# Weights loaded later, rows interleaved and heads finished one by one in a decode attention kernel

## The chip, the core and the metric

The kernel runs on one core of one Trainium2 chip. The metric is the device time of one execution in microseconds (us); the profile calls the stretch from the first to the last instruction the span. A median is taken over repeated runs, and a change counts as faster or slower when it moves the time by over 2%. In the profile PE is the matmul engine (PEld its weight loads), DVE the vector engine, ACT the scalar engine, SP the engine that issues most of the transfers, and a trailing q (DVEq, SPq) an engine's sequencer. L266 is line 266 of the kernel that is profiled, so the same operation has another line number in each variant.

## The reference

For each of two rows the output is the input, plus attention of one query token over a cache of 8192 keys in 32 heads of width 128, plus a gated MLP (gMLP). Inputs and outputs are bf16.

```python
# x (2,1,512); k_cache, v_cache (2,32,8192,128); wq (512,4096); wo (4096,512)
# w_in (512,1792); w_out (896,512)
xn = _layernorm(x)
q = heads(xn @ wq)
p = _softmax(einsum('bhqd,bhkd->bhqk', q, k_cache) * 128 ** -0.5)
attn = merge(einsum('bhqk,bhkd->bhqd', p, v_cache)) @ wo
z = _gelu(xn @ w_in);  z1, z2 = z[..., :896], _layernorm(z[..., 896:])
mlp = (z1 * (w_sp * z2 + b_sp)) @ w_out
out = x + attn + mlp
```

## The kernel before

Each head reads a K tile and a V tile of 2.10 MB each. DVE multiplies the whole K tile by the query, which stands broadcast in all partitions (`qbc`), and adds halves of the head dimension together, six times on the tile and once more into `s_t`. ACT takes the exponential, and PE multiplies by V in 64 small matmuls. The row is the outer loop, and the output projection waits for the end of each row. Below, heads are counted from 0 to 63 in the order in which they are worked on; `h` is the head index within a row.

```python
kpool = ctx.enter_context(tc.tile_pool(name="kpool", bufs=3))
vpool = ctx.enter_context(tc.tile_pool(name="vpool", bufs=2))
spool = ctx.enter_context(tc.tile_pool(name="spool", bufs=3))
# ... cut: wq chunks and the K/V pairs of heads 0 and 1 on the SyncE queue ...
nc.gpsimd.dma_start(w_in_sb[:], ...)      # 1.8 MB
nc.gpsimd.dma_start(w_out_sb[:], ...)     # 0.9 MB
nc.gpsimd.dma_start(wo_sb[:], ...)        # 4.2 MB, all heads
# ... cut: layer norm of x, helpers make_q and make_gmlp ...
make_q(0)
for b in range(B):
    o_ps = psum_ob.tile([P, H], F32, name="o_ps")
    for h in range(H):
        # ... cut: kt, vt = issue_kv(b, h), or the pair loaded ahead ...
        nc.vector.tensor_tensor(out=kt[:], in0=kt[:], in1=q_bcast, op=ALU.mult)
        w = Dh
        while w > 2:                      # six halving adds
            hw = w // 2
            nc.vector.tensor_tensor(out=kt[:, :, 0:hw], in0=kt[:, :, 0:hw],
                                    in1=kt[:, :, hw:w], op=ALU.add)
            w = hw
        s_t = spool.tile([P, J], F32, name="s_t")
        nc.vector.tensor_tensor(out=s_t[:].unsqueeze(2), in0=kt[:, :, 0:1],
                                in1=kt[:, :, 1:2], op=ALU.add)   # "the small add"
        e_t = spool.tile([P, J], BF16, name="e_t")
        nc.scalar.activation(out=e_t[:], in_=s_t[:], func=ACT.Exp, scale=SCALE,
                             accum_out=l_all[:, gh:gh + 1])
        for j in range(J):                # 64 value matmuls
            nc.tensor.matmul(o_ps[:, h:h + 1], lhsT=vt[:, j, :], rhs=e_t[:, j:j + 1], ...)
        if not prologue_done and (h >= 3 or h == H - 1):
            # ... cut: make_q of the other row, make_gmlp() ...
    # one block per row: sum over partitions, reciprocal, scaling,
    nc.tensor.matmul(l_ps[:], lhsT=ones_f[:], rhs=l_all[:, b * H:(b + 1) * H], ...)
    nc.vector.reciprocal(out=lr[:], in_=l_ps[:])
    nc.vector.tensor_tensor(out=o_sb[:, b, :], in0=o_ps[:], in1=lr[:], op=ALU.mult)
    # 7 matmuls with w_out, 32 with wo, the residual and the store
    # ... cut ...
```

The softmax here doesn't subtract the row's maximum and nothing guards it: scores larger than these inputs give would overflow.

## Time and profile before

| | kernel before |
|---|---|
| time, median (lowest to highest) of 6 runs | 727.93 us (724.26 to 729.3) |
| span of the profiled run (its time was 724.26) | 722.5 us |
| DVE busy | 641.7 us, 89% |
| multiply of one head, 128x8192 | 4.42 us |
| head to head, early / late | 10.15 / 10.21 us |

The prediction below shows the busy shares, the costliest groups, the timeline of DVE and the stretches. One further view helps. It is from the page: it divides the span into 40 equal slices, and gives DVE's busy share of each in tenths and the rate of the transfers.

```profile
DVE  2248899999999999999989899999999999999991
...
GB/s 304 356 390 283 424 429 429 426 427 427 415 403 411 422 421 385 423 423 402 403 409 208 432 424 433 424 430 422 399 408 412 414 414 409 405 424 401 418 228 0
```

DVE is idle for much of the first three slices (54 us) and in the last one.

### The profile page before, as it was taken

How to read it: one execution, taken by the hardware profiler on the slowest of the kernel's cores; microseconds unless marked ns; L12 is line 12 of the kernel's file. 1: busy time of each engine (PE TensorE's matmuls, PEld its weight loads, DVE VectorE, ACT ScalarE, POOL GpSimd, SP SyncE). 2: the span in 40 equal slices, each digit the busy share in tenths (PEclk: the TensorE clock that was granted, in tenths of full speed). 3: DMA queues.
4: the chain of work that ended last, by engine and by line, in shares of the span. 5: the costliest groups of instructions: out<-in, count | busy, mean ns of one | idle time of the engine just before them, and what ended most of it. 6: DMA issues, size and time to landing. Idle time of an engine off the chain costs nothing.

```text
span 722.5 us, 9759 instructions
## 1 busy us (share of the span) xinstructions
PE 163.1 (23%) x4303; PEld 133.2 (18%) x4304; DVE 641.7 (89%) x558; ACT 37.5 (5%) x151; POOL 5.4 (1%) x13
## 2 busy tenths in 40 slices
PE   0228412221222112211235221222112211222126
PEld 0004212221112112211222221221111111111012
DVE  2248899999999999999989899999999999999991
ACT  0004100000000000000000000000000000000000
POOL 2000000000000000000000000000000000000000
PEclk9999555555555555555557555555555555555557
DMA  7997999999999999999995999999999999999950
GB/s 304 356 390 283 424 429 429 426 427 427 415 403 411 422 421 385 423 423 402 403 409 208 432 424 433 424 430 422 399 408 412 414 414 409 405 424 401 418 228 0
DMA packets 24326, 280.21 MB, mean 388 GB/s; under 512 B 2294, under 2 KB 6396, under 8 KB 7900
## 3 DMA queue, kind: packets, MB, share of 16 engines
q1 hardware_dynamic: 22668, 272.64, 91.2%
q0 software_dynamic: 1616, 6.95, 2.7%
q8 instruction: 33, 0.54, 0.3%
q14 instruction: 9, 0.07, 0.0%
HBM read 279.58 MB, written 0.00 MB: 387 GB/s over the span
## 4 chain that ended last, share of the span: by engine, by line
DVE 80%; DMA 8%; PE 5%; SPq 4%; issue 2%; ACT 0%; DVEq 0%; ACTq 0%
DVE kt L270 43%; DVE kt L266 35%; DMA kt<-in_A_k_cache_dram 4%; DMA wq_sb<-in_A_wq_dram 4%; PE out_ps L311 2%; DVE s_t L275 2%; SPq L72 2%; PE q_ps L173 2%; SPq L81 1%; PE o_ps L284 1%; SPq L83 0%; DVE res L317 0%; ACT L279 0%; DVEq L275 0%; PE l_ps L295 0%
## 5 line engine op out<-in xcount | busy, mean ns | idle before, releaser
L270 DVE TENSOR_TENSOR kt<-kt 128x4096 bf16<-128x4096 bf16 (+5 forms) x384 | 335.6, 877 | 12.3
L266 DVE TENSOR_TENSOR kt<-kt,qbc 128x8192 bf16<-128x8192 bf16 x64 | 282.8, 4418 | 34.0 <-DMA kt<-in_A_k_cache_dram 22.1
L284 PE MATMUL o_ps<-e_t,vt 128*128 128x1 bf16 x4096 | 117.8, 165 | 509.0 <-ACT e_t L279 509.0
L284 PEld LDWEIGHTS <-vt 128*128 128x128 bf16 x4096 | 116.2, 104 | 512.4 <-issue 471.3
L279 ACT ACTIVATE e_t<-s_t 128x64 bf16<-128x64 f32 x64 | 16.4, 256 | 600.1 <-DVE s_t L275 600.1
L173 PE MATMUL q_ps<-wq_sb,xn_rep 128*128 128x512 bf16 x63 | 19.7, 470 | 22.5 <-DMA wq_sb<-in_A_wq_dram 22.4
L275 DVE TENSOR_TENSOR s_t<-kt 128x64 f32<-128x64 bf16 x64 | 19.1, 299 | 6.0
L311 PE MATMUL out_ps<-wo_sb,o_sb 128*1 128x512 bf16 x64 | 17.6, 443 | 1.4 <-DVE o_sb L299 1.4
L173 PEld LDWEIGHTS <-xn_rep 128*128 128x128 bf16 x64 | 6.6, 111 | 34.0 <-DMA wq_sb<-in_A_wq_dram 20.9
L279 ACT ACTIVATION_READ_ACCUMULATOR e_t<-s_t 128x1 f32 x64 | 11.9, 186 | 0.0
L177 ACT CAST qbc<-q_ps 128x512 bf16<-128x512 f32 x16 | 9.4, 585 | 46.5 <-PE q_ps L173 46.5
L317 DVE TENSOR_TENSOR res<-out_ps,x_b 1x512 bf16<-1x512 f32 x2 | 1.4, 678 | 9.8 <-PE out_ps L311 9.8
L311 PEld LDWEIGHTS <-o_sb 128*1 128x1 bf16 x64 | 5.9, 94 | 12.3 <-issue 5.1
L298 DVE RECIPROCAL lr<-l_ps 128x32 f32<-128x32 f32 x2 | 0.7, 358 | 5.7 <-PE l_ps L295 5.7
L305 PE MATMUL out_ps<-w_out_sb,hT 128*1 128x512 bf16 x14 | 4.8, 501 | 1.7 <-DVE hT L249 0.9
L184 PE MATMUL zst_ps<-xnT,w_in_sb 128*128 128x2 bf16 x56 | 1.9, 165 | 10.3 <-DMA w_in_sb<-in_B_w_in_dram 10.3
L184 PEld LDWEIGHTS <-w_in_sb 128*128 128x128 bf16 x56 | 1.8, 100 | 11.1 <-DMA w_in_sb<-in_B_w_in_dram 10.4
L279 ACT ACT_TABLE_LOAD x2 | 2.6, 1283 | 13.6 <-DVE s_t L275 13.6
L157 PE MATMUL zst_ps<-ident,xn_rows 2*128 2x2 f32 x4 | 0.6, 238 | 11.5 <-DVE xn_rows L147 11.5
L157 PEld LDWEIGHTS zst_ps<-ident,xn_rows 2*128 2x128 f32 x4 | 0.5, 208 | 11.5 <-issue 11.5
L233 DVE CAST wsp_f<-wsp_sb 128x1 f32<-128x1 bf16 x1 | 0.2, 154 | 2.5 <-DMA wsp_sb<-in_B_w_sp_dram 2.5
L124 DVE CAST x_f<-x_rows 2x512 f32<-2x512 bf16 x1 | 0.4, 415 | 2.1 <-DMA x_rows<-in_A_x_dram 2.1
(54 smaller groups left out, 21.9 us busy)
## 6 DMA issues: line engine op xcount, KB each, us to landing
kt<-in_A_k_cache_dram SPq DMA_DIRECT2D x64, 2048.0 KB, 14.7
vt<-in_A_v_cache_dram SPq DMA_DIRECT2D x64, 2048.0 KB, 9.5
wq_sb<-in_A_wq_dram SPq DMA_DIRECT2D x8, 512.0 KB, 22.4
wo_sb<-in_A_wo_dram POOLq DMA_DIRECT2D x1, 4096.0 KB, 36.4
w_in_sb<-in_B_w_in_dram POOLq DMA_DIRECT2D x1, 1792.0 KB, 19.8
w_out_sb<-in_B_w_out_dram POOLq DMA_DIRECT2D x1, 896.0 KB, 22.4
x_b<-in_A_x_dram SPq DMA_DIRECT2D x2, 1.0 KB
out_dram<-res SPq DMA_DIRECT2D x2, 1.0 KB
```

The costliest lines, as they stand in the source:

```text
L72: nc.sync.dma_start(wq_sb[:, :, c * NQ:(c + 1) * NQ], A_wq[:, c * NQ:(c + 1) * NQ].rearrange("(k p) n -> p k n", p=P),)
L81: nc.sync.dma_start(kt[:], A_k_cache[b, h].rearrange("(p j) d -> p j d", p=P))
L173: nc.tensor.matmul(q_ps[:], lhsT=xn_rep[:, b, k, :], rhs=wq_sb[:, k, c * NQ:(c + 1) * NQ], start=(k == 0), stop=(k == KD - 1),)
L177: nc.scalar.copy(out=qbc[b][:, c * NQ:(c + 1) * NQ], in_=q_ps[:])
L184: nc.tensor.matmul(z_ps[:, c, :], lhsT=w_in_sb[:, k, c * P:(c + 1) * P], rhs=xnT[:, k, :], start=(k == 0), stop=(k == KD - 1),)
L266: nc.vector.tensor_tensor(out=kt[:], in0=kt[:], in1=q_bcast, op=ALU.mult)
L270: nc.vector.tensor_tensor(out=kt[:, :, 0:hw], in0=kt[:, :, 0:hw], in1=kt[:, :, hw:w], op=ALU.add)
L275: nc.vector.tensor_tensor(out=s_t[:].unsqueeze(2), in0=kt[:, :, 0:1], in1=kt[:, :, 1:2], op=ALU.add)
L279: nc.scalar.activation(out=e_t[:], in_=s_t[:], func=ACT.Exp, scale=SCALE, accum_out=l_all[:, gh:gh + 1],)
L284: nc.tensor.matmul(o_ps[:, h:h + 1], lhsT=vt[:, j, :], rhs=e_t[:, j:j + 1], start=(j == 0), stop=(j == J - 1),)
L305: nc.tensor.matmul(out_ps[:], lhsT=hT[:, c, b:b + 1], rhs=w_out_sb[:, c, :], start=(idx == 0), stop=(idx == n_mm - 1),)
L311: nc.tensor.matmul(out_ps[:], lhsT=o_sb[:, b, h:h + 1], rhs=wo_sb[:, h, :], start=(idx == 0), stop=(idx == n_mm - 1),)
```

## The change

The intent is to take from the start what it doesn't need, and to spread the work of the tail over the heads:

1. `w_in` and `w_out` are no longer loaded at the start but at heads 4 and 8 of the loop, and `wo` comes as one tile of 131 KB per head index, all on the SyncE queue.
2. The head is the outer loop and the row the inner one; a query chunk is made for both rows at once.
3. K has four buffers instead of three, V three instead of two.
4. Each head is finished by itself under the multiply of the next: one matmul for the sum, a reciprocal of 128x1 on DVE, a scaling on ACT, one output matmul. Only seven `w_out` matmuls per row are left for the end.
5. DVE runs in program order (`manual_schedule`), where before the scheduler chose. The gMLP stands ahead of the two heads of h = 8.

```diff
-    kpool = ctx.enter_context(tc.tile_pool(name="kpool", bufs=3))
-    vpool = ctx.enter_context(tc.tile_pool(name="vpool", bufs=2))
+    kpool = ctx.enter_context(tc.tile_pool(name="kpool", bufs=4))
+    vpool = ctx.enter_context(tc.tile_pool(name="vpool", bufs=3))
+    wpool = ctx.enter_context(tc.tile_pool(name="wpool", bufs=3))
 ... cut ...
+    def issue_wo(h):
+        wt = wpool.tile([P, N_OUT], BF16, name="wot")
+        nc.sync.dma_start(wt[:], A_wo[h * Dh:(h + 1) * Dh, :])
+        return wt
 ... cut: order of the first loads ...
-    nc.gpsimd.dma_start(w_in_sb[:], B_w_in.rearrange("(k p) f -> p k f", p=P))
-    nc.gpsimd.dma_start(w_out_sb[:], B_w_out.rearrange("(c p) n -> p c n", p=P))
-    wo_sb = const.tile([P, H, N_OUT], BF16, name="wo_sb")
-    nc.gpsimd.dma_start(wo_sb[:], A_wo.rearrange("(h p) n -> p h n", p=P))
+    def issue_w_in_dma():
+        nc.sync.dma_start(w_in_sb[:], B_w_in.rearrange("(k p) f -> p k f", p=P))
+    def issue_w_out_dma():
+        nc.sync.dma_start(w_out_sb[:], B_w_out.rearrange("(c p) n -> p c n", p=P))
 ... cut ...
+    def finish_head(st, last):
+        b_, h_, gh_, hps_, wo_t_, out_ps_, first_ = st
+        rl = work.tile([P, 1], F32, name="rl")
+        nc.vector.reciprocal(out=rl[:], in_=hps_[:, 1:2])
+        nc.scalar.activation(out=o_sb[:, gh_:gh_ + 1], in_=hps_[:, 0:1], func=ACT.Copy,
+                             scale=rl[:, 0:1])
+        nc.tensor.matmul(
+            out_ps_[:], lhsT=o_sb[:, gh_:gh_ + 1], rhs=wo_t_[:],
+            start=first_, stop=False,
+        )
 ... cut: finish_row, the 7 w_out matmuls, residual and store ...
+    with tc.manual_schedule(engines={mybir.EngineType.DVE}):
         for h in range(H):
+            for b in range(B):
 ... cut ...
+                if b == 0 and h == 8:
+                    issue_w_out_dma()
+                if b == 0 and h == 4:
+                    issue_w_in_dma()
+                if b == 0 and h == 8:
+                    make_gmlp()
+                    prox.close()
+                nc.vector.tensor_tensor(out=kt[:], in0=kt[:], in1=q_bcast, op=ALU.mult)
+                if prev is not None:
+                    finish_head(prev, False)
 ... cut: the six adds, the small add, exp and value matmuls as before ...
+                nc.tensor.matmul(hps[:, 1:2], lhsT=ones_f[:], rhs=l_all[:, gh:gh + 1],
+                                 start=True, stop=True)
+        finish_head(prev, True)
+        finish_row(1, out_pss[1])
```

## The prediction

> **What bounds the kernel now.** I read the page's busy shares first, then the groups of instructions, then VectorE (DVE) in order of time, and last the DMA rate of single stretches.
>
> ```profile
> PE 163.1 (23%) x4303; PEld 133.2 (18%) x4304; DVE 641.7 (89%) x558; ACT 37.5 (5%) x151; POOL 5.4 (1%) x13
> ...
> L270 DVE TENSOR_TENSOR kt<-kt 128x4096 bf16<-128x4096 bf16 (+5 forms) x384 | 335.6, 877 | 12.3
> L266 DVE TENSOR_TENSOR kt<-kt,qbc 128x8192 bf16<-128x8192 bf16 x64 | 282.8, 4418 | 34.0 <-DMA kt<-in_A_k_cache_dram 22.1
> ```
>
> DVE works 641.7 of 722.5 us, nearly all of it on 64 equal heads (one multiply of 4.42 us, six halving adds, one last small add). The change leaves this work alone, so the 81 us in which DVE idles are the most that it could win. The timeline of DVE shows where the large idle pieces lie:
>
> ```profile
> 12.30 1.17 DVE L163 COPY xn_rep<-xnT 128x128 bf16<-128x128 bf16 x8
> 25.39 4.42 DVE L266 TENSOR_TENSOR kt<-kt,qbc 128x8192 bf16<-128x8192 bf16 x1 [11.92 <-ACT qbc L177]
> 46.34 4.42 DVE L266 TENSOR_TENSOR kt<-kt,qbc 128x8192 bf16<-128x8192 bf16 x1 [16.52 <-DMA kt<-in_A_k_cache_dram]
> 50.68 9.58 DVE L270 TENSOR_TENSOR kt<-kt 128x4096 bf16<-128x4096 bf16 x12
> 60.17 0.51 DVE L275 TENSOR_TENSOR s_t<-kt 128x64 f32<-128x64 bf16 x2
> 63.18 4.43 DVE L266 TENSOR_TENSOR kt<-kt,qbc 128x8192 bf16<-128x8192 bf16 x1 [2.50 <-DMA kt<-in_A_k_cache_dram]
> ...
> 706.53 0.30 DVE L275 TENSOR_TENSOR s_t<-kt 128x64 f32<-128x64 bf16 x1
> 709.68 0.36 DVE L298 RECIPROCAL lr<-l_ps 128x32 f32<-128x32 f32 x1 [2.85 <-PE l_ps L295]
> 710.07 0.19 DVE L299 TENSOR_TENSOR o_sb<-o_ps,lr 128x32 bf16<-128x32 f32 x1
> 719.57 0.68 DVE L317 TENSOR_TENSOR res<-out_ps,x_b 1x512 bf16<-1x512 f32 x1 [9.31 <-PE out_ps L311]
> ```
>
> Three pieces are to be seen. The start: the scheduler interleaved heads 0 and 1, head 0's adds stand behind head 1's multiply, that one waits for its K tile until 46.34, and the third multiply starts only at 63.18. The end: 15.7 us lie between the last add (706.83) and the end of the span, 9.2 of them 32 output matmuls in a row. In between all is steady: multiplies start 10.15 us apart (98.45 to 108.60) and later 10.21 (686.33 to 696.54). From 63.18 to 706.83 are 643.7 us; 62 heads at 10.21 are 633, so only 11 us are lost in the long middle: the gMLP, the change of row at 374 (about 4) and three short waits for K.
>
> The stretches (PE, PEld, DVE, ACT, POOL busy, then clock, DMA share, GB/s) show how close DMA is:
>
> ```profile
> 98.45:190.34 91.89, 16.60 (x576) 16.59 (x576) 89.25 (x74) 4.42 (x19) 0.00 (x0) 0.50 1.01 428
> 200.55:363.91 163.36, 29.53 (x1024) 29.02 (x1024) 158.42 (x129) 5.59 (x32) 0.00 (x0) 0.50 1.00 410
> 20.00:40.00 20.00, 6.09 (x29) 1.87 (x29) 4.42 (x1) 1.75 (x3) 0.00 (x0) 1.00 1.04 351
> 48.00:56.00 8.00, 3.21 (x9) 1.21 (x10) 8.00 (x4) 0.58 (x1) 0.00 (x0) 1.00 1.05 365
> ```
>
> While DMA catches up it moves 428 GB/s; once DVE sets the pace it moves what is asked for, 4.19 MB in 10.21 us, 410. Where wq and wo are loaded (rows of 1 KB) it falls to about 350. DVE is the bound, DMA a close second.
>
> **The Trainium skill.** *HBM Reference*, Specifications, puts a core streaming alone at about 425 GB/s; the trace agrees (428). *DMA: Bandwidth & Descriptors*, Specifications, gives 512 B as the smallest transfer for line rate; this trace does not bear that out for the 1 KB rows, 351 and 365 GB/s. *Perfetto Trace Analysis*, Optimization Strategy, says that consistent bubbles can mean too few buffers. The trace has none: the multiply waited for K four times in 64. So deeper pools alone should earn little. *VectorE: DVE Perf Modes*, The perf-mode tier table, has bf16 tensor_tensor capped at two elements per cycle; 8192 in 4.42 us agree with that at the 0.96 GHz of its Specifications, so the heads' time stays.
>
> **The change part by part.**
>
> *Start.* DVE now follows program order, so head 0 is not held by head 1. The queries come chunk by chunk for both rows, and w_in, w_out and wo leave the start for later. What then counts is the third K tile, behind two K/V pairs, all of wq (4.19 MB) and one wo tile: five 2.10 MB tiles at 428 GB/s, 24.5 us, and 4.3 MB of 1 KB rows. For the latter I take 315 GB/s: in the packet records a 1 KB packet takes about 52 ns, times 16 engines. That is 13.7 us. Data flow from about 5.3 us (1.18 MB had moved by 8.0), so the tile is there near 44. The same sum for the second K tile of the kernel before gives 46, and it came at 46.34. Heads 0 and 1 fit in ahead (start near 12, then K at 23.5, done by 34), and DVE waits some 10 us. Third multiply at 44 instead of 63.2: 19 us won.
>
> *A head in the middle.* Added per head: one reciprocal of 128x1, which by the rows of 128x2 (166 ns) takes about 0.16 us, 64 of them 10 us of busy time. It stands between the multiply and the first add. In the kernel before a copy of 0.18 us stood in the same place once (z_sb, 67.52) and the first add began 4.46 us after the multiply's start, exactly as without it. So I count zero, at most 0.06 for its second wait. The matmuls of the previous head must be through: exp, one matmul for the sum and 1.85 us of value matmuls end about 3 us into the head, the reciprocal asks at 4.4. ACT and PE have room. Taken: 10.18 us a head, 62 heads, 631 us.
>
> *gMLP.* It now stands on DVE as one block of 22 small operations ahead of head 16. The kernel before took 4.2 us from zsig to hT; with the five ahead of them, the exp round trip and two casts I take 6 us.
>
> *DMA in the middle.* Two heads need four tiles and one 131 KB wo tile: 19.6 + 0.4 us, 10.0 a head against 10.18. At head 2 DMA has no lead, by head 9 1.3 us, then w_in costs 4.4: DVE waits 3 us. The gMLP gives 6 back before w_out asks for 3. K now goes out three heads ahead, so no further wait.
>
> *Change of row.* Gone, 4 us; it is in the 11 us that I replace.
>
> *Tail.* Of 39 output matmuls, 8 stay behind the last head: 0.5 (exp) + 0.5 (sum) + 1.85 + 0.2 (reciprocal) + 0.4 (ACT) + 8 x 0.43 + 0.7 (residual) + 2.3 (store) = 10, instead of 15.7.
>
> Sum: 44 + 631 + 3 + 6 + 10 = 694 us of span. The median of the runs lay 5.4 us above the profiled span (727.93 against 722.5); I add 6: 700 us.
>
> **The rivals.** First: DMA becomes the bound. At 410 GB/s instead of 428 a head takes 10.4 us of DMA; then 61 heads from 44, w_in, w_out, one head on DVE and the tail give 44 + 636 + 7 + 10 + 10 = 707 of span, 712 in time. Against it: whenever DMA had a backlog it held 427 to 428 over some 100 us, twice. Second: the reciprocal makes DVE wait for PE and ACT in each head, say 0.3 us, 19 us in all: 718, a gain within 2%. The margin of 1.4 us at a granted clock of 0.50 speaks against it. Third: the early part is slower, because PE does all query chunks before head 1's value matmuls, so that the reciprocal in head 2 asks at 48.8 what PE gives near 47; a slip of a few us at most. Fourth: the 1 KB rows move at 365, and the third K tile comes at 42: 698.
>
> **Range and chances.** The start and the tail are arithmetic on measured rates and hold to 3 or 4 us each; the middle can only grow, by 0.1 us a head for every 1% of DMA. So 690 to 711. Faster by over 2% means below 713.4: 0.93; within 2% 0.06; slower 0.01.
>
> **What would show it.** Right: third multiply at 42 to 47, released by DMA; multiplies 10.15 to 10.25 apart; idle ahead of the reciprocals near zero; one DVE wait of some us near head 9; 10 us from last add to end. Wrong: DMA waits ahead of multiplies all through, then DMA is the bound; PE or ACT as releaser of the reciprocals, then the second rival; a third multiply after 50.

## The result and the profile after

| | before | after |
|---|---|---|
| time, median (lowest to highest) | 728.32 us (724.26 to 729.97), 16 runs | 694.07 us (693.59 to 694.26), 8 runs |
| profiled span | 722.5 us | 692.2 us |
| third multiply starts | 63.18 us | 44.27 us |
| third multiply to end of last small add | 643.65 us | 638.07 us |
| end of last small add to end of span | 15.7 us | 9.86 us |

The changed kernel takes 0.9535 of the time, with a 95% interval of 0.9517 to 0.9552. Such a ratio is the mean time of one kernel's fast runs over that of the other's in the same rounds, so it is not quite the ratio of the medians quoted.

The last three rows of the table divide the 30.3 us by which the span shrank: 18.9 at the start, 5.6 in the middle and 5.8 in the tail. (The medians differ by 34.3 us, because the profiled run of the kernel before was its fastest.)

The page of the kernel after gives these shares and DVE groups. A group's line gives busy time, the mean ns of one, and after the second bar the idle time ahead of it with what ended most of it.

```profile
PE 213.4 (31%) x4427; PEld 157.6 (23%) x4428; DVE 645.4 (93%) x618; ACT 54.3 (8%) x215; POOL 2.5 (0%) x11
...
L320 DVE TENSOR_TENSOR kt<-kt 128x4096 bf16<-128x4096 bf16 (+5 forms) x384 | 336.9, 877 | 11.0
L313 DVE TENSOR_TENSOR kt<-kt,qbc 128x8192 bf16<-128x8192 bf16 x64 | 282.8, 4418 | 18.3 <-DMA kt<-in_A_k_cache_dram 15.0
...
L274 DVE RECIPROCAL rl<-hps 128x1 f32<-128x1 f32 x64 | 10.2, 160 | 2.3 <-PE hps L339 2.3
```

Each multiply and add lasts what it lasted before. The idle time ahead of the multiplies fell from 34.0 to 18.3 us. The new reciprocals add 10.2 us of busy time, yet DVE is busy only 3.7 us longer, as records that overlap are counted once. The timeline of DVE, with start, duration and, in brackets, the wait before it, shows the start, the wait at head 9, two heads of the steady part and the tail:

```profile
23.61 4.42 DVE L313 TENSOR_TENSOR kt<-kt,qbc 128x8192 bf16<-128x8192 bf16 x1 [1.05 <-DMA kt<-in_A_k_cache_dram]
...
44.27 4.43 DVE L313 TENSOR_TENSOR kt<-kt,qbc 128x8192 bf16<-128x8192 bf16 x1 [10.42 <-DMA kt<-in_A_k_cache_dram]
48.61 0.16 DVE L274 RECIPROCAL rl<-hps 128x1 f32<-128x1 f32 x1
...
118.84 4.42 DVE L313 TENSOR_TENSOR kt<-kt,qbc 128x8192 bf16<-128x8192 bf16 x1 [3.50 <-DMA kt<-in_A_k_cache_dram]
...
226.06 4.42 DVE L313 TENSOR_TENSOR kt<-kt,qbc 128x8192 bf16<-128x8192 bf16 x1
...
236.20 4.42 DVE L313 TENSOR_TENSOR kt<-kt,qbc 128x8192 bf16<-128x8192 bf16 x1
240.53 0.16 DVE L274 RECIPROCAL rl<-hps 128x1 f32<-128x1 f32 x1
240.65 5.43 DVE L320 TENSOR_TENSOR kt<-kt 128x4096 bf16<-128x4096 bf16 x6
...
682.04 0.30 DVE L325 TENSOR_TENSOR s_t<-kt 128x64 f32<-128x64 bf16 x1
...
685.24 0.17 DVE L274 RECIPROCAL rl<-hps 128x1 f32<-128x1 f32 x1 [2.31 <-PE hps L339]
689.36 0.68 DVE L289 TENSOR_TENSOR res<-out_ps,x_b 1x512 bf16<-1x512 f32 x1 [3.96 <-PE out_ps L284]
```

The third multiply still waits for its K tile, but only until 44.27. In the steady part a head takes 10.14 us (226.06 to 236.20), and the first add begins 4.45 us after the multiply (236.20 to 240.65) though a reciprocal stands in between. The stretch view, in the columns that the prediction names, shows the transfers in the steady part:

```profile
236.00:640.00 404.00, 115.15 (x2680) 91.53 (x2680) 395.95 (x357) 24.49 (x120) 0.00 (x0) 0.50 1.01 426
```

At 426 GB/s the transfers are within half a per cent of the 428 seen before the change, and DVE is busy 98% of this stretch. Both are near the highest figures seen in these stretches, and no multiply of the stretch waits for K.

### The profile page after: what moved, and what is told of

Its sections match the earlier page's. It is cut to its first block, busy times and chain, and to the rows that moved or that the text cites. A ratio compares the mean times of both kernels' runs of the same rounds, so it can differ in the third digit from the quotient of the medians.

```text
span 692.2 us, 10168 instructions
## 1 busy us (share of the span) xinstructions
PE 213.4 (31%) x4427; PEld 157.6 (23%) x4428; DVE 645.4 (93%) x618; ACT 54.3 (8%) x215; POOL 2.5 (0%) x11
## 4 chain that ended last, share of the span: by engine, by line
DVE 74%; issue 13%; DMA 6%; SPq 4%; PE 1%; ACT 0%; DVEq 0%; ACTq 0%
DVE kt L320 45%; DVE kt L313 25%; DMA kt<-in_A_k_cache_dram 6%; SPq L76 4%; DVE s_t L325 3%; DVE rl L274 1%; PE hps L339 0%; PE out_ps L284 0%; SPq L86 0%; PE hps L336 0%; SPq L88 0%; ACT e_t L331 0%; DVE res L289 0%; SPq L93 0%; PE out_ps L277 0%
## 5 line engine op out<-in xcount | busy, mean ns | idle before, releaser
L313 DVE TENSOR_TENSOR kt<-kt,qbc 128x8192 bf16<-128x8192 bf16 x64 | 282.8, 4418 | 18.3 <-DMA kt<-in_A_k_cache_dram 15.0
L336 PE MATMUL hps<-l_all,ones_f 128*128 128x1 f32 x128 | 37.0, 358 | 328.3 <-ACT e_t L331 328.3
L339 PEld LDWEIGHTS <-vt 128*128 128x128 bf16 x4096 | 125.8, 107 | 0.0
L339 PE MATMUL hps<-e_t,vt 128*128 128x1 bf16 x4096 | 117.9, 165 | 0.0
L336 PEld LDWEIGHTS hps<-l_all,ones_f 128*128 128x128 f32 x128 | 31.7, 307 | 360.9 <-ACT e_t L331 360.8
L277 PE MATMUL out_ps<-wot,o_sb 128*1 128x512 bf16 x64 | 37.3, 583 | 131.2 <-ACT o_sb L275 128.9
L275 ACT ACTIVATE o_sb<-hps,rl 128x1 bf16<-128x1 f32 x64 | 16.9, 263 | 257.3 <-DVE rl L274 257.3
L185 PE MATMUL q_ps<-wq_sb,xn_rep 128*128 128x512 bf16 x63 | 21.8, 516 | 9.4 <-DMA wq_sb<-in_A_wq_dram 7.9
L274 DVE RECIPROCAL rl<-hps 128x1 f32<-128x1 f32 x64 | 10.2, 160 | 2.3 <-PE hps L339 2.3
L284 PE MATMUL out_ps<-w_out_sb,hT 128*1 128x512 bf16 x14 | 6.4, 631 | 0.0
```

Source lines behind the costliest of these rows:

```text
L185: nc.tensor.matmul(q_ps[:], lhsT=xn_rep[:, b, k, :], rhs=wq_sb[:, k, c * NQ:(c + 1) * NQ], start=(k == 0), stop=(k == KD - 1),)
L274: nc.vector.reciprocal(out=rl[:], in_=hps_[:, 1:2])
L275: nc.scalar.activation(out=o_sb[:, gh_:gh_ + 1], in_=hps_[:, 0:1], func=ACT.Copy, scale=rl[:, 0:1])
L277: nc.tensor.matmul(out_ps_[:], lhsT=o_sb[:, gh_:gh_ + 1], rhs=wo_t_[:], start=first_, stop=False,)
L336: nc.tensor.matmul(hps[:, 1:2], lhsT=ones_f[:], rhs=l_all[:, gh:gh + 1], start=True, stop=True)
L339: nc.tensor.matmul(hps[:, 0:1], lhsT=vt[:, j, :], rhs=e_t[:, j:j + 1], start=(j == 0), stop=(j == J - 1),)
```

## The experiments

Eleven runs were made, ten of new kernels and one of the kernel before (e10), and all gave correct results. "Theory A" and "theory B" are those of each run's expectation. The kernel before was run beside them. The median of its runs was 727.6 to 728.8 us in each set. The changed kernel was not run again beside them: differences against it are taken from its eight runs above, and no ratio with an interval exists for them.

### e1: the kernel before in program order

This does one part alone: DVE's order is fixed, all else is as before.

```diff
-    for b in range(B):
+    with tc.manual_schedule(engines={mybir.EngineType.DVE}):
+        for b in range(B):
 ... the loop's body indented, otherwise unchanged ...
```

> The kernel before, with one edit: VectorE keeps program order in the loop over heads, so that head 0's adds no longer stand behind head 1's multiply. Theory A (the order of the loads sets the start): the third K tile is issued and lands as before, the third multiply starts near 63 as before (63.18), and the time stays at 726 to 730 us. Theory B (the step of my prediction that says that head 0 is no longer held by head 1): the third multiply starts by 57 and the time falls by 6 us or more, to 722 or less.

The time was 732.14 us, ratio 1.0072 (1.0035 to 1.0108). The timeline of DVE:

```profile
46.17 4.42 DVE L267 TENSOR_TENSOR kt<-kt,qbc 128x8192 bf16<-128x8192 bf16 x1 [10.72 <-DMA kt<-in_A_k_cache_dram]
...
63.09 4.42 DVE L267 TENSOR_TENSOR kt<-kt,qbc 128x8192 bf16<-128x8192 bf16 x1 [6.67 <-DMA kt<-in_A_k_cache_dram]
...
387.71 0.68 DVE L318 TENSOR_TENSOR res<-out_ps,x_b 1x512 bf16<-1x512 f32 x1 [9.59 <-PE out_ps L312]
```

Head 0 is now done long before head 1 begins, and still the third multiply starts at 63.09 instead of 63.18. The interleaving of heads 0 and 1 had only filled a wait for K. At the change of row, program order even costs time: the residual of row 0 stands ahead of the next head, and DVE waits 9.59 us for it, where the scheduler had put other work first and waited 0.54. Theory A held; the loss was somewhat above its range.

### e2: the change with the scheduler's order

```diff
-    with tc.manual_schedule(engines={mybir.EngineType.DVE}):
+    if True:
```

> The changed kernel without the fixed order on VectorE: the scheduler puts each head's reciprocal behind the same head's last add, ahead of the next multiply. Theory A: there it waits for exp, the sum and the 64 value matmuls of the same head, as the last head's does in the changed kernel (2.31 us idle, 2.9 from the end of the last add to its start); 62 times 2.9 plus 0.16 us make about 190 us, so 870 to 890 us, multiplies 13.1 us apart. Theory B (deeper pools and the order of the loads are the change, the place of a 0.16 us operation is nothing): 694 to 700 us.

The time was 879.1 us, ratio 1.2092 (1.2047 to 1.2137). The group of reciprocals and two heads of the timeline:

```profile
L274 DVE RECIPROCAL rl<-hps 128x1 f32<-128x1 f32 x64 | 10.7, 168 | 189.9 <-PE hps L339 189.9
```

```profile
61.51 0.17 DVE L274 RECIPROCAL rl<-hps 128x1 f32<-128x1 f32 x1 [2.83 <-PE hps L339]
61.59 4.41 DVE L313 TENSOR_TENSOR kt<-kt,qbc 128x8192 bf16<-128x8192 bf16 x1
...
74.70 0.17 DVE L274 RECIPROCAL rl<-hps 128x1 f32<-128x1 f32 x1 [2.90 <-PE hps L339]
```

The scheduler put each reciprocal ahead of the next multiply, not behind it. DVE then waits some 2.9 us in every head for ACT and PE, and a head takes 13.19 us (61.51 to 74.70). So fixing the order is no gain by itself (e1), but it is what makes finishing each head affordable. Theory A held.

### e3: the change with the old buffer counts

```diff
-    kpool = ctx.enter_context(tc.tile_pool(name="kpool", bufs=4))
-    vpool = ctx.enter_context(tc.tile_pool(name="vpool", bufs=3))
+    kpool = ctx.enter_context(tc.tile_pool(name="kpool", bufs=3))
+    vpool = ctx.enter_context(tc.tile_pool(name="vpool", bufs=2))
```

> The changed kernel with the pools of the kernel before (3 K tiles and 2 V tiles in place of 4 and 3). Theory A (start and tail made the gain; K tiles rarely were late before): 696 to 700 us, third multiply at 44 as now, the wait at w_in a few us longer. Theory B (the depth of the pools made the gain): 715 us or more, with DMA waits ahead of many multiplies.

The time was 693.72 us, ratio 0.9541 (0.9502 to 0.958), the same as the change itself. The third multiply started at 44.53 and the wait at head 9 was 3.48 us. The deeper pools earn nothing, still less than theory A gave them. (The reverse, deeper pools in the kernel before, does not fit into the on-chip memory.)

### e4: the change with the gMLP's weights loaded early

```diff
     def issue_w_in_dma():
-        nc.sync.dma_start(w_in_sb[:], ...)
+        nc.gpsimd.dma_start(w_in_sb[:], ...)
 ... the same for w_out, and both called at once ...
+    issue_w_in_dma()
+    issue_w_out_dma()
```

> The changed kernel, but w_in and w_out (2.75 MB) are loaded at the start from the GpSimd queue, as in the kernel before; wo stays one tile per head. Theory A (every byte ahead of the third K tile delays all that follows): third multiply at 51 to 52 instead of 44.3, the 3.5 us wait near head 9 goes, so 697 to 699 us. Theory B (the loads at the start are hidden behind heads 0 and 1): third multiply near 44.3, and 690 to 691 us because the wait near head 9 goes.

The time was 703.05 us, ratio 0.9673 (0.964 to 0.9707): some 9 us of the gain are gone, twice what theory A expected. The third multiply started at 56.98, without waiting for K. What held it stands in the timelines of DVE and then of PE:

```profile
25.38 4.42 DVE L312 TENSOR_TENSOR kt<-kt,qbc 128x8192 bf16<-128x8192 bf16 x1 [16.63 <-ACT qbc L192]
...
51.22 0.17 DVE L277 RECIPROCAL rl<-hps 128x1 f32<-128x1 f32 x1 [11.27 <-PE hps L338]
```

```profile
22.38 0.61 PE L199 MATMUL zst_ps<-xnT,w_in_sb 128*128 128x2 bf16 x17 [15.04 <-DMA w_in_sb<-in_B_w_in_dram]
22.86 5.83 PE L188 MATMUL q_ps<-wq_sb,xn_rep 128*128 128x512 bf16 x16
```

PE, whose order the scheduler still chose, took the gMLP's matmuls ahead of the first query matmuls and waited there 15.04 us for `w_in`. So the first query came late. Later PE did 48 query matmuls ahead of most of head 1's value matmuls, and the reciprocal in DVE's fixed order waited 11.27 us. The run therefore mixes two things, the bytes at the start and PE's order. It shows a trap, but doesn't give a price for the early bytes alone.

### e5: the kernel before with the weights loaded late

This is the cleaner test of the bytes: the order of heads, the scheduler and the tail stay as they were. Only the other row's queries and the gMLP move from h = 3 to h = 6, where their weights have come.

```diff
-    nc.gpsimd.dma_start(w_in_sb[:], ...)
-    nc.gpsimd.dma_start(w_out_sb[:], ...)
-    nc.gpsimd.dma_start(wo_sb[:], ...)
 ... in the loop, on the SyncE queue ...
+            if b == 0 and h == 4:
+                issue_w_in()
+            if b == 0 and h == 6:
+                issue_w_out()
+            if b == 0 and h % 2 == 0 and 8 <= h < 24:
+                issue_wo((h - 8) // 2)        # four heads' rows of wo
-            if not prologue_done and (h >= 3 or h == H - 1):
+            if not prologue_done and (h >= 6 or h == H - 1):
```

> The kernel before, with only the loads of w_in, w_out and wo (6.95 MB) moved from the start to the SyncE queue inside the first row (heads 4, 6, and wo in eight pieces from head 8 on); pools, loop order, tail and the scheduler's choice stay. Theory A (the bytes ahead of the third K tile are the gain at the start): third multiply at 44 to 46 instead of 63, time 707 to 712 us, about 18 us less than before; tail and period stay as before. Theory B (loop order, pools and fixed order are needed for it): third multiply after 50, time 715 us or more.

The time was 714.69 us, ratio 0.9809 (0.9795 to 0.9824), which is unclear by the 2% rule. The timeline of DVE:

```profile
43.62 4.43 DVE L282 TENSOR_TENSOR kt<-kt,qbc 128x8192 bf16<-128x8192 bf16 x1 [6.34 <-DMA kt<-in_A_k_cache_dram]
```

The third multiply starts 19.6 us sooner than in the kernel before. So the later weights alone give the whole gain of the start. But the time fell by only 14 us, so 5 to 6 are lost again: the way from the third multiply to the end of the last small add takes 653.4 us, 9.8 more than in the profile before, which was itself the fastest of its runs. The waits account for part: 3.8 for the gMLP's first matmuls, some 1.7 more for K and 1.4 more for the residual of row 0. Some 2 us more are the gMLP's small operations: here they stand as one block and cost 5.2 us besides that wait (63.99 to 83.20, less a head of 10.21), where the kernel before had some of them inside heads and lost 3.2 (63.18 to 88.30, less two heads and a wait for K). The rest, about 1 us, stays open. The tail took 16.1 us, about as before. The result lies between the two theories, at 14 of the 18 us.

### e6: the change with a shorter tail

The seven `w_out` matmuls of row 1 are moved ahead of the last head's output matmul.

```diff
                 if h == H - 1 and b == B - 1:
+                    row_mlp(0, out_pss[0], True)
                     finish_row(0, out_pss[0])
+                    row_mlp(1, out_pss[1], False)
```

> The changed kernel, but the seven w_out matmuls of the last row are issued during the last head, ahead of its value matmuls, so that one output matmul stays at the end. Theory A (these seven are on the path that sets the end, 7 x 0.43 us): the end comes 2.5 to 3.2 us earlier, 691 to 691.6 us. Theory B (PE is held up by the 14 matmuls that now stand ahead of the value matmuls and gives the gain back): 693 to 694.5 us.

The time was 691.32 us, ratio 0.9486 (0.9472 to 0.95), 2.75 us below the changed kernel's median. The timeline of DVE:

```profile
686.85 0.68 DVE L291 TENSOR_TENSOR res<-out_ps,x_b 1x512 bf16<-1x512 f32 x1 [0.97 <-PE out_ps L277]
```

The wait for the output matmuls fell from 3.96 to 0.97 us, and the tail from 9.86 to 6.9. Output matmuls behind the last head count in full: the tail really is a chain. Theory A held.

### e7: the change with wq in pieces

Only the first of the eight chunks of wq is loaded at the start. The others come one by one in the loop, each ahead of the heads that need it.

```diff
-    for c in range(1, min(2, NQC)):
-        issue_wq(c)
-    for c in range(2, NQC):
-        issue_wq(c)
 ... in the loop ...
+                if b == 0 and h % 4 == 2 and h // 4 + 1 < NQC:
+                    issue_wq(h // 4 + 1)
+                if b == 0 and h % 4 == 3 and h // 4 + 1 < NQC:
+                    make_q_chunk(h // 4 + 1)
```

> The changed kernel, but only the first wq piece is loaded at the start; the other seven go out one by one, each two heads of both rows ahead of its use. Theory A (DMA is a close second bound: what is taken from the start must be moved later): third multiply near 33 instead of 44.3, but then multiplies wait for K tiles again and again, 9 to 12 us in all after head 2, and the time is 687 to 690 us. Theory B (only the start counts, DMA has room in the middle): few waits after head 2, 683 to 685 us.

The time was 687.82 us, ratio 0.9441 (0.9427 to 0.9455). The group of multiplies:

```profile
L310 DVE TENSOR_TENSOR kt<-kt,qbc 128x8192 bf16<-128x8192 bf16 x64 | 282.8, 4419 | 11.4 <-DMA kt<-in_A_k_cache_dram 11.4
```

The multiply of head 2 no longer waits: at 43.12 head 3 begins. The idle time ahead of multiplies falls from 18.3 to 11.4 us, and the time by 6.3. The bytes removed from the start return in part: after head 3 there are six waits for K, 7.8 us in all (the longest 4.11 at 109.55), where the changed kernel has one of 3.50. That is why a wait of 10.42 us gave only 6. Theory A's time held, though it expected more of these waits.

### e8: the change with two reciprocals per head

A second, unused reciprocal stands behind the first.

```diff
         nc.vector.reciprocal(out=rl[:], in_=hps_[:, 1:2])
+        rl2 = work.tile([P, 1], F32, name="rl2")
+        nc.vector.reciprocal(out=rl2[:], in_=hps_[:, 1:2])
```

> The changed kernel with a second, unused reciprocal behind the first one in each head, to learn how much room there is between the multiply and the first add. Theory A (the gap holds just one small operation: the first add starts 4.46 us after the multiply with and without one): the second costs 0.11 to 0.2 us a head, 63 heads, 7 to 12 us, time 701 to 706 us. Theory B (small operations there are free): 694 to 695 us.

The time was 694.95 us, ratio 0.9537 (0.9521 to 0.9553). The timeline of DVE:

```profile
236.69 4.42 DVE L315 TENSOR_TENSOR kt<-kt,qbc 128x8192 bf16<-128x8192 bf16 x1
241.03 0.16 DVE L274 RECIPROCAL rl<-hps 128x1 f32<-128x1 f32 x1
241.11 0.15 DVE L276 RECIPROCAL rl<-hps 128x1 f32<-128x1 f32 x1
241.17 5.42 DVE L322 TENSOR_TENSOR kt<-kt 128x4096 bf16<-128x4096 bf16 x6
```

The first add starts 4.48 us after the multiply, against 4.45 with one reciprocal. So 64 more reciprocals of 0.15 us, 9.5 us of busy time, cost at most 0.9 us. Between a multiply and an add that needs its result there is a gap that DVE can't use for that add, and an independent small operation fits into it almost for nothing. Theory B held. Busy time is a bad price for such an operation.

### e9: the kernel before with its own pool for s_t

This run asks why a head takes 10.15 us early and 10.21 later in the kernel before. With 40 buffers the small add needn't wait for ACT to be done with an old `s_t` until late.

```diff
+    stpool = ctx.enter_context(tc.tile_pool(name="stpool", bufs=40))
-            s_t = spool.tile([P, J], F32, name="s_t")
+            s_t = stpool.tile([P, J], F32, name="s_t")
```

> The kernel before with 40 buffers for the scores in place of 3, so that the small last add needs no wait for ScalarE in the first 43 heads. Theory A (that second wait, which the changed kernel has under the multiply instead, is what makes a head 10.21 us long rather than 10.14): multiplies 10.14 apart up to head 43 and 10.21 after it, 2 to 3 us less in all, 725 to 727 us where the kernel before has 728 to 729. Theory B (the period has another cause, for instance DMA): 10.21 stays and so does the time.

One run, the profiled one (761.06 us, clock 1.0), isn't used for the time. The three fast runs took 723.11 to 725.32 us, ratio 0.9953 (0.9908 to 0.9997), somewhat below theory A's range. The view of one line's instructions, for the small add of the kernel before, of e9, and last for the reciprocal of the kernel after (duration ns, first and last start us):

```profile
L275 DVEq EVENT_SEMAPHORE  x57: 21/21/21, 128.7 to 706.5; - x57
```

```profile
L276 DVEq EVENT_SEMAPHORE  x20: 21/21/21, 538.8 to 732.8; - x20
```

```profile
L274 DVEq EVENT_SEMAPHORE  x60: 21/21/21, 57.3 to 685.2; - x60
```

In the kernel before, 57 small adds have an extra semaphore instruction ahead of them, from 128.7 on. In the same, fast profile the head that begins at 108.60, without one, takes 10.13 us, and the next takes 10.21:

```profile
118.73 4.42 DVE L266 TENSOR_TENSOR kt<-kt,qbc 128x8192 bf16<-128x8192 bf16 x1
...
128.94 4.42 DVE L266 TENSOR_TENSOR kt<-kt,qbc 128x8192 bf16<-128x8192 bf16 x1
```

In e9 only 20 have one. Its profile is of the slow run, but there too a head takes 10.14 us where there is none (359.17 to 369.31) and 10.21 where there is (600.30 to 610.51). So a second wait in front of the small add costs about 0.07 us, and 57 of them some 4.0 us by this estimate. The 37 that e9 removes would make 2.6 us; its fast runs gained 3.4 (0.2 to 6.7), so the time agrees but could not show it alone. Theory A's account of the period held. In the kernel after, no small add has one: 60 stand ahead of the reciprocals, inside the gap that e8 measured. That the reciprocal's wait for PE makes the other one needless is my reading of the code; the count is what the trace shows.

### e10: the kernel before once more

> The kernel before once more, unchanged. Its runs scatter over 724 to 730 us, those of the changed kernel over less than 1 us, and my prediction took the difference between its median and the profiled span as a fixed 6 us. Theory A (the scatter is waits of VectorE for K tiles or PE in the middle): a profile of some other time differs from the first one by waits in the middle, while start and tail are the same. Theory B (a fixed cost outside the span): the time minus the span differs from the 1.8 us of the first profile.

The kernel is unchanged. One run gave 727.45 us with a span of 725.7, so the time was 1.75 us above the span, as in the first profile (724.26 and 722.5). The start was the same (third multiply at 62.97). Of the 3.2 us between the two profiles, 2.65 lie in the middle: a wait for K of 2.59 instead of 1.58 us near 89, and a wait for the residual of row 0 of 2.08 instead of 0.54. The tail was 0.8 us longer (the wait for the output matmuls 10.07 instead of 9.31), which theory A did not expect. So the scatter of the kernel before comes, in these two profiles, mostly from its waits in the middle, partly from the tail, and is no fixed cost. What makes those waits vary stays open.

### e11: both improvements together

The short tail of e6 and wq in pieces, here as the first chunk and then four transfers of up to two chunks each (rows of 2 KB), at every eighth head index.

```diff
+                if b == 0 and h % 8 == 2:
+                    issue_wq(h // 4 + 1, 2)
+                if b == 0 and h % 4 == 3 and h // 4 + 1 < NQC:
+                    make_q_chunk(h // 4 + 1)
 ... and the edit of e6 ...
```

> Both improvements together: the wq pieces late as in the seventh experiment, but in four DMAs with rows of 2 KB, and the short tail of the sixth. Theory A (start, DMA and tail add up as separate terms): 687.8 less 2.7 for the tail and up to 1 for the longer rows, 683.5 to 686 us, faster than both kernels. Theory B (larger pieces come later and make the multiplies wait longer): 687 us or more.

The time was 684.55 us (683.66 to 684.82), ratio 0.9411 (0.9371 to 0.9451). Of DVE's waits:

```profile
DVE kt L313 <- DMA kt<-in_A_k_cache_dram: 7.7, 5, 3.8
...
DVE res L286 <- PE out_ps L272: 1.0, 1, 1.0
```

The two gains add up: the waits for K are down to 7.7 us from 15.0, those for the output matmuls to 1.0 from 4.0. This version is faster than the kernel before. It is 1.4% below the changed kernel: less than the 2% that counts, but all its runs lie at least 8.7 us below all runs of that kernel. Theory A held.

## Why the prediction was right, step by step

The prediction said 700 us and 690 to 711; the time was 694.07. The direction, the sizes of the parts and the remaining waits came as worked out.

**Start.** Predicted 44, measured 44.27, released by DMA. The byte count was the right argument. e5 shows the cause: the later weights alone bring it to 43.62. That 44 was hit so closely is partly luck, for two terms were off in opposite directions. Where almost only rows of 1 KB moved (28 to 36 us), the rate was 349 GB/s and not the 315 taken, which makes 1.3 us less. And by 44.2 us 15.95 MB had moved, 1.1 MB more than the sum counts, or some 2.6 us at 428 GB/s. One sentence of that step was wrong as a reason, that head 0 "is not held by head 1" any more. e1 fixes only the order and gains nothing. This did not enter the sum, since the third K tile sets the start in either case.

**A head in the middle.** Predicted 10.18, measured 10.14. The mechanism was right, the reciprocal is free (e8), and with one exception, the last, no reciprocal waited. The term was sized a little too high. It allowed up to 0.06 us for the reciprocal's second wait. That wait is there (60 semaphore instructions in e9's last line) but lies in the gap. And it overlooked that the 10.21 of the later heads held a second wait at the small add, which the change removes. Over 62 heads that is some 2.5 us (62 times 0.04).

**Waits and gMLP.** Predicted 3 us near head 9 and 6 for the gMLP. Measured: 3.50 at 118.84, and 5.83 from the gMLP's first operation at 189.82 to the next multiply at 195.65. No further wait of note came. The reason given, that K now goes out three heads ahead, was not needed: with the old pools (e3) none came either.

**The middle as a whole.** The 62 heads at 10.135 (54.44 to 64.59 is 10.15, 226.06 to 236.20 is 10.14), the wait and the gMLP make 637.7 us, and 638.07 were measured. Of the 5.6 us gained against before, about 4.0 are by e9's estimate the second waits, which the prediction did not name. The other 1.6 are the change of row, which had cost 4.5 (363.75 to 388.70 is 24.95 for two heads of 10.21), and other small waits, less the new wait and the gMLP's block. (Of the "three short waits for K" that the prediction saw in the middle, there were two, 1.58 at 88.30 and 1.47 at 400.46; the third ends where the middle begins.) The row order was not tested alone.

**Tail.** Predicted 10, measured 9.86, in the predicted order: the 32 output matmuls that had taken 9.2 us are gone, the remaining seven take 3.19. No run gave the kernel before this tail alone: the 5.8 us are read from the two profiles, and e6 supports it.

**From span to time.** The sum of the steps was 694 us of span, and 692.2 were measured. The mis-sized term is the 6 us added to come to a time. It was read off as the median of the kernel before less one profiled span, but the profiled run happened to be its fastest. Time less span of one and the same run is 1.8 us (694.01 and 692.2 after, 727.45 and 725.7 in e10). The other 3.6 were scatter, which the kernel after hardly has: its eight runs lie within 0.7 us. With 1.8 the prediction would have been 696.

**The rivals.** DMA as the bound did not come true: the rate held at 426 GB/s and the steady part had no waits. (That rival's 636 us for 61 heads of 10.4 should be 634.) The reciprocal waiting for PE and ACT is a real danger, shown by e2, but the change's fixed order averts it. A slow early part by query chunks ahead of head 1's value matmuls did not appear (the reciprocal at 48.61 has no wait), while e4 shows how it looks when it does. The fourth, a third tile at 42, was off by 2 us, though its reason was sound: the 349 GB/s measured are nearer to its 365 than to the 315 of the sum. That the pools would earn little held; e3 shows no gain at all.

## What to carry to other kernels

Before the first steady iteration, count the bytes that stand ahead of the first few tiles, and move out whatever isn't needed yet: here that was 19 of the 30 us. Per-iteration finishing work on the busiest engine is nearly free if it lies in a gap between two dependent operations one iteration later, and very expensive one place earlier, so fix its place in the program instead of leaving it to a scheduler. To turn a span into a time, take both from the same run.

## What the Trainium skill lacked or had wrong

- *DMA: Bandwidth & Descriptors*, Specifications, puts the smallest transfer for line rate at 512 B. Stretches of the kernel before with many 1 KB rows moved 351 and 365 GB/s, and one of the kernel after with almost nothing else (28 to 36 us) 349, against 428 in stretches of large rows.
- *VectorE: DVE Perf Modes*, The TRN2 errata, gives one fixed cost per instruction: in its table 120 cycles and the elements for a source in PSUM, and some 150 cycles measured for a copy within SBUF (estimates from these for one element at its 0.96 GHz: 0.126 and 0.157 us). The record of the 128x1 reciprocal, 0.16 us, agrees with the second figure, though its source is in PSUM. But two in a row start 0.08 us apart (e8), and behind a large multiply the first delays the next dependent add by nothing measurable and the second by 0.03 us. One cost per instruction does not tell these cases apart.
- *Perfetto Trace Analysis*, Identifying Dependency Chains, says that an instruction waiting on several engines may get extra EventSemaphore instructions; the trace has such instructions (57 in the kernel before). It gives no cost. Here the record lasts 0.021 us but the head becomes 0.07 us longer, and nothing is lost where the instruction lies in a gap.
- No page that I used warns that a scheduler may put a cheap dependent operation ahead of a long independent one: in e2 that cost 185 us.
